# A hand-ordered transformer block on one core: bias load moved to another queue, eleven warm-ups, more softmax buffers, a new order of all steps

## The chip, the cores and the metric

The kernel runs on one core of a Trainium2 chip. The metric is device time in microseconds (us) of one execution; the median of several executions is compared. Before the change the median of three runs is 173.74 us (173.52 to 173.78).

The engines are PE (TensorE, matmuls into the eight PSUM banks), DVE (VectorE), ACT (ScalarE), POOL (GpSimd) and SP (SyncE, which here only issues DMAs). Each works through its own queue in order and waits on semaphores for the others.

## The reference

Two branches share one layer norm of `x` (2048 tokens, 512 wide) and are added to it. Weights and activations are bf16.

```python
xn = (x - mean) / sqrt(var + 1e-5)

# branch A: linear attention, 32 heads of 16, feature maps from two softmaxes
q, k, v = split(xn @ wqkv)
pq, pk  = q @ w_phi, k @ w_phi                      # per head, 16x16
phi_q   = concat([softmax(pq), softmax(-pq)])
phi_k   = concat([softmax(pk), softmax(-pk)])
kv, z   = phi_k^T v, sum(phi_k)                     # per head
o       = (phi_q @ kv) / (phi_q . z + 1e-6)
A       = o @ wo

# branch B: dense, mish, dense (hidden width 1792)
h   = xn @ w1 + b1
B   = (h * tanh(softplus(h))) @ w2

out = x + A + B
```

## The kernel before

The 2048 tokens are 16 tiles of 128, in four groups of four. `xnT` holds the normalised tokens turned, so that they can be the stationary or the moving operand of the projections. `w_phi` is folded into the weights of k and q on the chip: `wT`, the turned slice of `wqkv`, comes by a DMA transpose (L143), and 16 small matmuls per slice (F0 for k, F for q, L156) multiply it by the block-diagonal `Wbd`. Attention works in two passes: `s` from 0 to 3 for the keys of the four token groups, 4 to 7 for the queries.

All work is cut into steps, and one string, `STEPS` (L24), lists them in the order in which the kernel emits them; nothing else reorders them. Since each engine's queue runs in order, `STEPS` sets the order on each engine, and the order of DMAs on SP. `@b` names the PSUM bank that a step's result takes; a bank is free again when the copy that reads it has run. `a` or `v` at the end of a step says whether ACT or DVE does it. The steps that matter here:

- `LS i`, `RS i`, `AZ i`, `TP i`, `TC i`: the first token group tile by tile. Statistics on DVE (L170, L172), reciprocal root on POOL (L176, L177), normalise on DVE (L181), four transposes on TensorE (L560), copy to `xnT` (L565).
- `LN g`, `AP g k`: statistics and root of a later group; then two tiles normalised on DVE and one DMA transpose issued on SP for them (L186), which writes their part of `xnT`. The text calls such a DMA transpose a turn.
- `F0 kt`, `FD kt`: fold of k's weights and copy to `wkp`. `F`, `FC`: the same for q into `wqp`. `WT` loads the second `wT`.
- `LP`: the first two tiles' key logits, eight matmuls (L209). `L s i` one tile's logits (L194), `WL i` the same into a spare bank pair, `LC s i` the copy into `p_sb` (L252).
- `V t`, `VC t`: values of a tile (L194) and copy into `vext` (L218).
- `H u`, `M u`: a 128x512 block of the hidden layer (L228), mish with bias `b1f` on ACT (L239). Fourteen blocks per token group: H 0 to 13 belong to the first, H 14 to 27 to the second.
- `PB`, `CB`: the bias arrives as 14 rows of 128 in `b1b`; PB turns it on TensorE (L533), CB copies it to `b1f` (L605). All mish steps read `b1f`.
- `E s 0/1`: running maximum or minimum over 16 entries and the difference (L263 to L272, DVE). `X s k`: exponentials (L288, ACT). `S s k`: sums (L305, DVE). `R s k`: reciprocal of the sums, on DVE (L334, L335) or as exp(-ln) on ACT (L322, L314). `N s k`: normalise (L340). `A g k`: accumulate kv (L387). For queries `W s k` weighs and turns (L345), `Q`, `G`, `C` attend, gather and divide.
- `O t`, `P t`, `Y t`: second dense layer (L463), output projection (L470), residual and store (L477, L478). `OH`, `PH`, `YH`: the last tile in two parts.
- `DX g` loads a token group, `DW 2` and `DW 3` load `w2` and `wo`; all on SP.

Before the steps, DMAs are issued by hand: on SP the first x tile, `wT`, x tiles 2 and 3, `wv`, the first half of `w1`, x tiles 4 to 7, the second half of `w1`; on ACT `w_phi`, x tile 1 and the bias. Then twelve warm-up matmuls on constants (L512) keep TensorE busy while loads arrive.

The softmax sums `s` have 3 buffers (L304), `r2` has 2 (the pool's default), and logarithms go to a tile of their own (L318).

Of the kernel before, what the change touches and what calls it, by code (L numbers as in the profile page):

```python
# [21 lines left out]
STEPS = """  # L24
LS 0; RS 0; DX 2; LS 1; WB; RS 1; AZ 0; TP 0 @0; F0 0 @1; F0 1 @2; AZ 1; FD 0 v; TP 1 @3; TC 1 v; LS
2; PB @4; RS 2; TC 0 a; LS 3; RS 3; FD 1 a; AZ 2; F0 2 @5; F0 3 @0; FD 2 a; FD 3 a; LP i @1,2; KM;
DX 3; AZ 3; V 0 @3; LC 0 0 a; TP 2 @5; V 1 @0; TC 2 a; TP 3 @1; VC 0 a; LC 0 1 v; TC 3 v; CB; L 0 2
@5; L 0 3 @2; LC 0 3 a; LN 1; H 0 @3; H 1 @1; H 2 @4; M 0; LC 0 2 a; H 3 @2; M 1; M 2; M 3; VC 1 a;
E 0 0; H 4 @3; H 5 @5; AP 1 0; H 6 @1; H 7 @4; M 4; H 8 @2; M 5; H 9 @0; M 6; M 7; H 10 @3; M 8; M
9; M 10; AP 1 1; H 11 @5; E 0 1; V 4 @1; X 0 1; WL 1; LN 2; V 6 @4; VC 4 a; X 0 0; L 1 0 @2; L 1 3  # L30
@0; LC 1 0 a; V 5 @3; LN 3; VC 5 a; H 12 @1; WL 2; H 13 @2; VC 6 a; S 0 0; LC 1 3 a; M 11; V 3 @3; M
12; M 13; H 14 @4; H 15 @0; H 16 @5; H 17 @1; VC 3 a; M 14; H 18 @2; M 15; M 16; M 17; LC 1 2 a; H
19 @3; AP 2 0; AP 2 1; AP 3 0; L 2 0 @4; LC 2 0 a; L 2 1 @0; LC 2 1 a; V 2 @5; S 0 1; L 2 2 @1; M
18; LC 1 1 a; M 19; H 20 @4; LC 2 2 a; AP 3 1; H 21 @0; WT; H 22 @2; M 20; VC 2 a; R 0 1 v; L 2 3
@3; H 23 @1; R 0 0 v; N 0 1; M 21; N 0 0; H 24 @4; M 22; LC 2 3 a; F 0 @5; F 1 @0; E 1 0; E 1 1; M
23; M 24; F 2 @2; E 2 0; E 2 1; FC 0 a; H 25 @3; H 26 @1; FC 1 a; H 27 @4; M 25; M 26; L 3 2 @5; FC
2 a; M 27; V 7 @0; L 3 3 @3; V 11 @1; F 3 @2; L 3 0 @4; LC 3 0 v; LC 3 2 a; L 3 1 @5; A 0 0; X 1 0;
X 1 1; A 0 1; LC 3 3 a; FC 3 v; S 1 0; V 8 @4; LC 3 1 a; VC 7 a; L 4 0 @2; E 3 0; VC 8 a; LC 4 0 a;
L 4 1 @3; LC 4 1 a; L 4 3 @5; VC 11 a; L 4 2 @0; X 2 0; V 9 @4; L 5 0 @2; H 28 @3; H 29 @1; VC 9 a;
LC 4 2 v; M 28; M 29; H 30 @0; H 31 @4; H 32 @3; M 30; H 33 @1; H 34 @0; M 31; M 32; M 33; M 34; H  # L40
35 @4; M 35; H 36 @3; M 36; S 1 1; LC 4 3 a; R 1 0 v; E 3 1; LC 5 0 a; N 1 0; R 1 1 v; H 37 @1; H 38
@0; H 39 @4; H 40 @3; H 41 @5; H 42 @2; S 2 0; A 1 0; M 37; N 1 1; M 38; M 39; M 40; A 1 1; M 41; M
42; X 3 0; L 6 3 @1; L 5 2 @0; V 10 @4; VC 10 a; L 5 1 @3; LC 5 2 a; L 6 0 @5; E 4 0; E 4 1; X 2 1;
S 3 0; V 15 @2; VC 15 a; V 13 @4; VC 13 a; LC 6 0 a; R 2 0 a; S 2 1; DW 3; R 3 0 a; X 3 1; L 6 1 @0;
LC 5 1 a; DW 2; N 3 0; N 2 0; L 5 3 @2; O 0 @4; S 3 1; V 12 @5; V 14 @3; LC 6 1 a; LC 5 3 a; O 1 @0;
L 6 2 @2; R 2 1 a; N 2 1; VC 14 a; LC 6 3 a; VC 12 v; R 3 1 a; N 3 1; X 4 0; A 2 0; S 4 0; LC 6 2 a;
A 2 1; A 3 0; W 4 0 v; X 4 1; H 43 @3; M 43; A 3 1; H 44 @1; H 45 @5; M 44; H 46 @2; M 45; H 47 @3;
M 46; M 47; H 48 @1; KV; H 49 @5; H 50 @2; Q 0 0; M 48; M 49; G 0 0; M 50; H 51 @3; H 52 @1; H 53
@5; S 4 1; W 4 1 v; M 51; M 52; H 54 @2; H 55 @3; Q 0 1; M 53; E 5 0; E 5 1; M 54; E 6 0; L 7 0 @1;
M 55; G 0 1; C 0 a; X 5 0; LC 7 0 a; L 7 1 @5; X 5 1; O 2 @2; O 3 @3; LC 7 1 a; L 7 2 @1; LC 7 2 a;  # L50
S 5 0; Q 1 0; L 7 3 @5; G 1 0; E 6 1; W 5 0 a; P 0; P 1; Y 0; Q 1 1; O 4 @1; G 1 1; LC 7 3 a; O 5
@4; S 5 1; Q 2 0; O 6 @5; C 1 a; P 2; G 2 0; W 5 1 v; Y 1; Q 2 1; P 3; O 7 @0; E 7 0; X 6 0; S 6 0;
G 2 1; Q 3 0; C 2 a; G 3 0; Y 2; Y 3; X 6 1; O 8 @2; Q 3 1; W 6 0 v; E 7 1; S 6 1; P 4; P 5; G 3 1;
C 3 a; Q 4 0; X 7 0; Y 4; W 6 1 v; X 7 1; S 7 0; O 9 @3; O 10 @1; G 4 0; Q 4 1; P 6; P 7; G 4 1; Y
5; Y 6; C 4 a; Q 5 0; W 7 0 a; G 5 0; O 11 @4; Q 5 1; Y 7; O 12 @5; S 7 1; G 5 1; C 5 a; Q 6 0; G 6
0; O 13 @0; Q 6 1; G 6 1; W 7 1 v; P 8; P 9; Q 7 0; C 6 a; G 7 0; P 10; P 11; Y 8; Q 7 1; G 7 1; O
14 @2; Y 9; Y 10; C 7 a; P 12; P 13; OH 0 @3; PH 0; Y 11; P 14; OH 1 @1; PH 1; Y 12; Y 13; YH 0; Y
14; YH 1
"""


# [1 line left out]
def kernel(  # L63
# [424 lines left out]
    nc.scalar.dma_start(b1b[:], b1_v[:, :])  # L488
# [167 lines left out]
```

## Time and profile before

| what | value |
| --- | --- |
| median of 3 runs | 173.74 us |
| the profiled execution's own time | 174.0 us |
| its span (first to last instruction or landing on the core) | 172.3 us |
| DVE: sums of exponentials (L305) | 36.4 us busy, 16 of 2.28 us |
| ACT: mish (L239) | 37.2 us busy, 56 of 0.69 us |
| ACT: table loads (L138, L495) | 8 of 1.28 us |
| DMA: x, the three 512 KB loads, issue to landing | median 10.0 us |
| DMA: turns of xn, issue to landing | 3.3 us |

The granted TensorE clock is 1.0 in the profile's record over the whole span. An instruction's duration is longer than the distance to the next one where an engine pipelines: a 128x512 matmul lasts 0.379 us, and the next one starts 0.216 us after it; a 128x512 copy on ACT lasts 0.587 us, and the next one can start 0.48 us after it.

### The profile page before, as it was taken

The page shows a single profiled execution, that of the slowest core. Times are in us where ns is not written, and L with a number is a line of the kernel's source. Part 1 is how long each engine was busy: PE and PEld are TensorE (multiplying, and loading weights), DVE is VectorE, ACT ScalarE, POOL GpSimd, SP SyncE. Part 2 cuts the span into 40 slices and gives each one's busy share as a digit, 9 for nine tenths or more (in the row PEclk, how much of TensorE's full clock was granted, in tenths as well). Part 3 has the DMA queues.
Part 4 walks back from the last instruction along what each step waited for, and adds up shares of the span by engine and source line. Part 5 has one row for each costly group of instructions (what it writes and reads, how often), then busy time and mean ns, then how long its engine had stood idle before and what let it go on. Part 6 is the DMA issues. An engine that isn't in the chain of part 4 may idle for free.

```text
span 172.3 us, 2713 instructions
## 1 busy us (share of the span) xinstructions
PE 168.7 (98%) x1039; PEld 82.4 (48%) x1039; DVE 143.2 (83%) x221; ACT 119.5 (69%) x192; POOL 9.4 (5%) x26
## 2 busy tenths in 40 slices
PE   8999999999999999999999999999999999999993
PEld 2554444444545444454446544444444545445452
DVE  2878998999997999979999999799988996844433
ACT  2446889979899998989999988974063883414200
POOL 4332205000000000000000000000000000000000
PEclk9999999999999999999999999999999999999999
DMA  5999350199930000000000363023974749885641
GB/s 98 269 377 365 82 98 0 37 189 207 366 120 0 0 4 0 0 0 0 4 0 0 64 118 66 12 51 67 150 152 93 150 95 144 172 168 100 173 134 61
DMA packets 44953, 18.02 MB, mean 105 GB/s; under 512 B 37004, under 2 KB 44940, under 8 KB 44940
## 3 DMA queue, kind: packets, MB, share of 16 engines
q1 hardware_dynamic: 44096, 17.60, 44.5%
...
q8 instruction: 8, 0.13, 0.3%
q14 instruction: 5, 0.04, 0.1%
...
## 4 chain that ended last, share of the span: by engine, by line
PE 95%; DMA 3%; SPq 0%; DVE 0%; issue 0%
PE po L463 28%; PE ph L228 28%; PE pl L194 14%; PE po L470 8%; PE pv L194 8%; DMA wT<-in_A_wqkv_dram 3%; PE pnd L418 2%; PE pkv L387 2%; PE pfold L156 1%; PE pwide L194 1%; PE pl L209 1%; PE ptr L560 0%; SPq L483 0%; DVE x_sb L477 0%; PE pb L533 0%
## 5 line engine op out<-in xcount | busy, mean ns | idle before, releaser
L463 PE MATMUL po<-w_sb,acts 128*128 128x512 bf16 (+2 forms) x238 | 50.7, 366 | 0.0
L228 PE MATMUL ph<-xnT,w_sb 128*128 128x512 bf16 x224 | 50.1, 379 | 0.0
L239 ACT ACTIVATE acts<-ph,b1f 128x512 bf16<-128x512 f32 x56 | 37.2, 694 | 4.6 <-PE ph L228 4.4
L305 DVE TENSOR_REDUCE s<-e 128x128 f32<-128x2048 bf16 x16 | 36.4, 2279 | 2.5 <-ACT e L288 2.5
L228 PEld LDWEIGHTS <-w_sb 128*128 128x128 bf16 x224 | 21.7, 98 | 25.5
L463 PEld LDWEIGHTS <-acts 128*128 128x128 bf16 x238 | 22.3, 98 | 24.1
L288 ACT ACTIVATE e<-e 128x2048 bf16<-128x2048 bf16 x16 | 30.3, 1908 | 0.0
L194 PEld LDWEIGHTS <-xnT 128*128 128x128 bf16 x184 | 17.6, 98 | 20.1 <-DMA wv<-in_A_wqkv_dram 0.2
L252 ACT CAST p_sb<-pl 128x512 bf16<-128x512 f32 x27 | 15.4, 587 | 5.5 <-PE pl L194 4.7
L433 ACT COPY ds<-pnd 128x32 f32<-128x32 f32 x16 | 2.9, 183 | 23.5 <-PE pnd L418 23.5
L194 PE MATMUL pv<-wv,xnT 128*128 128x512 bf16 x64 | 16.1, 379 | 0.0
L477 DVE TENSOR_TENSOR x_sb<-po,x_sb 128x512 bf16<-128x512 f32 (+2 forms) x17 | 10.9, 654 | 5.7 <-PE po L470 5.7
L470 PE MATMUL po<-wqk,xnT 128*128 128x512 bf16 (+2 forms) x68 | 15.5, 366 | 0.0
L194 PE MATMUL pl<-wqk,xnT 128*128 128x512 bf16 x64 | 15.3, 379 | 0.0
L170 DVE BATCH_NORM_STATS2 stats<-x_sb 128x6 f32<-128x512 bf16 x16 | 10.1, 679 | 4.3 <-DMA x_sb<-in_A_x_dram 4.3
L263 DVE TENSOR_TENSOR m<-m 128x512 bf16<-128x512 bf16 (+1 forms) x32 | 11.5, 358 | 1.1
L194 PE MATMUL pl<-wkp,xnT 128*128 128x512 bf16 x48 | 11.7, 379 | 0.0
L263 DVE TENSOR_TENSOR m<-p_sb 128x1024 bf16<-128x1024 bf16 x16 | 10.9, 682 | 0.2 <-ACT p_sb L252 0.2
L272 DVE TENSOR_TENSOR e<-p_sb,m 128x2048 bf16<-128x2048 bf16 x8 | 9.8, 1226 | 1.4 <-PE pkv L387 1.1
L272 DVE TENSOR_TENSOR e<-m,p_sb 128x2048 bf16<-128x2048 bf16 x8 | 9.8, 1225 | 0.3
L340 DVE TENSOR_TENSOR e<-e,r 128x2048 bf16<-128x2048 bf16 x8 | 9.6, 1215 | 0.0
L138 ACT ACT_TABLE_LOAD x7 | 9.0, 1283 | 0.1
...
## 6 DMA issues: line engine op xcount, KB each, us to landing
...
x_sb<-in_A_x_dram SPq DMA_DIRECT2D x3, 512.0 KB, 10.0
...
```

Source lines behind the costliest of these rows:

```text
L170: nc.vector.bn_stats(stats[:, i, :], xs[:, i, :])
L194: nc.tensor.matmul(pp, lhsT=xnT[:, t, kt, :], rhs=w[:, kt, :], start=(kt == 0), stop=(kt == KT - 1),)
L228: nc.tensor.matmul(ph_of[u][:], lhsT=w1_sb[:, kt, f * P : (f + 1) * P], rhs=xnT[:, g * TPG : (g + 1) * TPG, kt, :], start=(kt == 0), stop= ...
L239: nc.scalar.activation(acts[:, f, g * 512 : (g + 1) * 512], ph_of.pop(u)[:], ACT.Mish, bias=b1f[:, f : f + 1])
L252: copy(p_of[s][:, i, :], pl_of.pop((s, i)))
L263: nc.vector.tensor_tensor(out=m[:], in0=src[:, :, 0:half], in1=src[:, :, half : 2 * half], op=op)
L272: nc.vector.tensor_tensor(out=e_of[s][:].rearrange("p t j l c -> p (t j) l c")[:, :, pl, :].rearrange("p t (c e o) -> p t c e o", e=8, o=2 ...
L288: nc.scalar.activation(v, v, ACT.Exp)
L305: nc.vector.reduce_sum(t[:], pair(s, k).rearrange("p t j l (c e) -> p (t j l c) e", e=16), axis=AX.X)
L463: nc.tensor.matmul(po_of[t, c.stop][:, c], lhsT=acts[:, f, t * P : (t + 1) * P], rhs=w2_sb[:, f, c], start=(f == 0), stop=False,)
L470: nc.tensor.matmul(po_of[t, c.stop][:, c], lhsT=oT_of[t // 2][:, t % 2 * 4 + j, :], rhs=wo_sb[:, j, c], start=False, stop=(j == 3),)
L477: nc.vector.tensor_tensor(out=y, in0=po_of.pop((t, c.stop))[:, c], in1=y, op=ALU.add)
```

## The change

Four edits, and with them a new `STEPS` string:

- the load of `b1b` goes from ACT's queue to SP's, between the first half of `w1` and x tiles 4 to 7;
- `WARM` is 11 instead of 12;
- `s` has 6 buffers, `r2` 3, and DVE's `r` 1;
- `log` writes its result over its input instead of a tile of its own (called by `invert`, `weigh`, `combine`);
- `STEPS`: every step occurs as often as before, in another order, with other banks, and some copies, reciprocals and weighings on the other engine. Shown are the opening up to the second group's logits, and the end.

```diff
-WARM = 12
+WARM = 11
 STEPS = """
-LS 0; RS 0; DX 2; LS 1; WB; RS 1; AZ 0; TP 0 @0; F0 0 @1; F0 1 @2; AZ 1; FD 0 v; TP 1 @3; TC 1 v; LS
-2; PB @4; RS 2; TC 0 a; LS 3; RS 3; FD 1 a; AZ 2; F0 2 @5; F0 3 @0; FD 2 a; FD 3 a; LP i @1,2; KM;
-DX 3; AZ 3; V 0 @3; LC 0 0 a; TP 2 @5; V 1 @0; TC 2 a; TP 3 @1; VC 0 a; LC 0 1 v; TC 3 v; CB; L 0 2
-@5; L 0 3 @2; LC 0 3 a; LN 1; H 0 @3; H 1 @1; H 2 @4; M 0; LC 0 2 a; H 3 @2; M 1; M 2; M 3; VC 1 a;
-E 0 0; H 4 @3; H 5 @5; AP 1 0; H 6 @1; H 7 @4; M 4; H 8 @2; M 5; H 9 @0; M 6; M 7; H 10 @3; M 8; M
-9; M 10; AP 1 1; H 11 @5; E 0 1; V 4 @1; X 0 1; WL 1; LN 2; V 6 @4; VC 4 a; X 0 0; L 1 0 @2; L 1 3
...
+LS 0; LS 1; RS 0; AZ 0; TP 0 @0; WB; F0 0 @1; RS 1; AZ 1; TP 1 @2; F0 1 @3; FD 0 a; TC 0 v; F0 2 @4;
+FD 1 a; FD 2 a; TC 1 v; LS 2; F0 3 @5; FD 3 v; LP i @0,1; LS 3; RS 2; LC 0 0 a; RS 3; V 1 @2; AZ 2;
+TP 2 @3; AZ 3; V 0 @4; TP 3 @5; DX 2; TC 2 a; L 0 2 @0; VC 0 a; PB @3; TC 3 v; L 0 3 @4; VC 1 a; H 0
+@5; LC 0 3 a; H 1 @2; CB; LC 0 2 a; M 0; M 1; H 2 @3; M 2; LN 1; LN 2; AP 1 0; AP 1 1; H 3 @4; H 4
+@0; H 5 @5; AP 2 0; H 6 @2; M 3; H 7 @3; M 4; M 5; M 6; M 7; DX 3; LC 0 1 a; E 0 0; E 0 1; H 8 @4; H
+9 @0; M 8; H 10 @5; H 11 @2; H 12 @3; AP 2 1; H 13 @1; M 9; H 14 @4; M 10; M 11; M 12; L 1 0 @0; M
+13; V 3 @5; M 14; X 0 1; LN 3; L 2 0 @2; S 0 1; LC 1 0 v; X 0 0; WL 1; S 0 0; L 2 1 @3; V 2 @1; WL
+2; L 2 2 @4; LC 2 0 a; LC 2 1 a; LC 2 2 a; VC 3 a; H 15 @2; H 16 @3; R 0 1 a; AP 3 0; L 2 3 @0; M
...
+@2; C 7 v; OH 0 @5; P 12; P 13; PH 0; P 14; OH 1 @1; PH 1; Y 11; Y 12; Y 13; YH 0; Y 14; YH 1
 """
@@ sums
-        t = s_of[s, k] = smx.tile([P, 128], FP32, name="s", bufs=3)
+        t = s_of[s, k] = smx.tile([P, 128], FP32, name="s", bufs=6)
@@ log
-    def log(src, n):
+    def log(v):
 
         table("natural_log_exp_and_others")
-        t = smx.tile([P, 128], FP32, name="log")
-        nc.scalar.activation(t[:, 0:n], src, ACT.Ln)
-        return t[:, 0:n]
+        nc.scalar.activation(v, v, ACT.Ln)
+        return v
@@ invert
-        r2 = r_of[s, k] = smx.tile([P, 128, 2], BF16, name="r2")
+        r2 = r_of[s, k] = smx.tile([P, 128, 2], BF16, name="r2", bufs=3)
         if how == "a":
-            power(r2[:], log(t[:], 128), 128, -1.0)
+            power(r2[:], log(t[:]), 128, -1.0)
             return
-        r = smx.tile([P, 128], BF16, name="r")
+        r = smx.tile([P, 128], BF16, name="r", bufs=1)
@@ DMAs ahead of the steps
     nc.scalar.dma_start(x_sb[:, 1, :], x_v[:, 1, :])
-    nc.scalar.dma_start(b1b[:], b1_v[:, :])
     nc.sync.dma_start(x_sb[:, 2:4, :], x_v[:, 2:4, :])
     nc.sync.dma_start(wv[:], wqkv_v[:, :, 2 * D : 3 * D])
     nc.sync.dma_start(w1_sb[:, :, 0 : 7 * P], w1_v[:, :, 0 : 7 * P])
+    nc.sync.dma_start(b1b[:], b1_v[:, :])
     nc.sync.dma_start(x_sb[:, 4:8, :], x_v[:, 4:8, :])
     nc.sync.dma_start(w1_sb[:, :, 7 * P : F], w1_v[:, :, 7 * P : F])
```

In the new order `WB` (the block-diagonal weights, on DVE, L524) stands behind `AZ 0`; the key folds' copies go to ACT for kt 0 to 2 and to DVE for kt 3; `PB` stands between `L 0 2` and `L 0 3`; `LN 2` stands ahead of `AP 1`; and SP issues x tiles 12 to 15 (`DX 3`) behind the turns of `AP 1 0`, `AP 1 1` and `AP 2 0`.

More of the change, by code (lines that the diff above doesn't have):

```diff
@@ L30 @@
-9; M 10; AP 1 1; H 11 @5; E 0 1; V 4 @1; X 0 1; WL 1; LN 2; V 6 @4; VC 4 a; X 0 0; L 1 0 @2; L 1 3
[L31 to L58, printed above, removed]
+LS 0; LS 1; RS 0; AZ 0; TP 0 @0; WB; F0 0 @1; RS 1; AZ 1; TP 1 @2; F0 1 @3; FD 0 a; TC 0 v; F0 2 @4;
+FD 1 a; FD 2 a; TC 1 v; LS 2; F0 3 @5; FD 3 v; LP i @0,1; LS 3; RS 2; LC 0 0 a; RS 3; V 1 @2; AZ 2;
@@ new lines @@
+2; L 2 2 @4; LC 2 0 a; LC 2 1 a; LC 2 2 a; VC 3 a; H 15 @2; H 16 @3; R 0 1 a; AP 3 0; L 2 3 @0; M
+15; L 1 3 @4; AP 3 1; LC 2 3 a; LC 1 2 a; LC 1 3 a; H 17 @5; H 18 @2; H 19 @0; H 20 @4; E 2 0; N 0
+1; WT; R 0 0 v; M 16; LC 1 1 a; M 17; M 18; M 19; H 21 @3; H 22 @5; M 20; M 21; H 23 @2; M 22; M 23;
+H 24 @0; M 24; H 25 @4; H 26 @3; H 27 @5; H 28 @2; M 25; M 26; M 27; V 6 @0; VC 2 a; E 1 0; M 28; V
+5 @4; F 0 @3; E 1 1; F 1 @5; VC 6 a; F 2 @1; FC 0 a; FC 2 a; VC 5 v; H 29 @2; M 29; E 2 1; FC 1 a; V
@@ new lines @@
+9 @0; X 1 0; F 3 @4; V 10 @3; FC 3 v; N 0 0; L 3 3 @1; L 3 0 @2; X 1 1; V 8 @5; LC 3 0 v; V 7 @4; VC
+7 a; A 0 0; A 0 1; VC 10 a; V 4 @2; S 1 0; L 4 0 @4; X 2 0; VC 4 a; LC 3 3 v; LC 4 0 v; VC 9 a; S 1
+1; R 1 0 a; L 4 2 @3; LC 4 2 a; N 1 0; L 3 2 @1; LC 3 2 a; L 3 1 @4; LC 3 1 v; L 4 1 @2; L 4 3 @0; R
+1 1 v; VC 8 a; H 30 @3; H 31 @1; LC 4 3 v; H 32 @5; H 33 @4; N 1 1; X 2 1; M 30; A 1 0; M 31; E 3 0;
+S 2 0; S 2 1; M 32; M 33; H 34 @0; M 34; V 13 @3; VC 13 a; H 35 @1; H 36 @5; H 37 @4; H 38 @0; M 35;
@@ new lines @@
+M 36; M 37; LC 4 1 a; E 3 1; H 39 @3; M 38; H 40 @1; H 41 @5; M 39; H 42 @4; H 43 @2; M 40; M 41; M
+42; M 43; H 44 @0; DW 2; M 44; A 1 1; E 4 0; V 14 @3; V 11 @1; E 4 1; X 3 1; L 5 0 @5; LC 5 0 a; X 3
+0; L 5 3 @4; LC 5 3 a; R 2 1 a; O 0 @2; S 3 1; R 2 0 a; L 5 1 @0; VC 14 a; LC 5 1 a; N 2 1; VC 11 a;
+V 15 @5; VC 15 a; R 3 1 a; L 6 3 @4; S 3 0; O 1 @3; L 6 0 @0; V 12 @1; X 4 0; L 5 2 @5; N 3 1; LC 6
+0 a; R 3 0 a; N 2 0; VC 12 a; L 6 1 @0; N 3 0; LC 6 3 a; A 2 0; S 4 0; LC 5 2 a; W 4 0 v; A 2 1; DW
@@ new lines @@
+3; X 4 1; S 4 1; A 3 0; H 45 @1; A 3 1; KM; LC 6 1 a; H 46 @4; L 6 2 @5; M 45; KV; M 46; H 47 @0; H
+48 @1; M 47; LC 6 2 a; H 49 @4; M 48; M 49; W 4 1 v; H 50 @0; H 51 @5; M 50; E 5 0; M 51; E 5 1; H
+52 @1; H 53 @4; H 54 @0; M 52; M 53; E 6 0; M 54; Q 0 0; G 0 0; H 55 @5; L 7 2 @1; Q 0 1; M 55; G 0
+1; L 7 0 @4; O 2 @0; X 5 0; S 5 0; C 0 a; W 5 0 v; Q 1 0; G 1 0; O 3 @5; LC 7 0 a; LC 7 2 a; Q 1 1;
+L 7 1 @4; G 1 1; C 1 a; O 4 @1; LC 7 1 a; E 6 1; X 5 1; O 5 @4; S 5 1; P 0; Q 2 0; G 2 0; X 6 0; P
@@ new lines @@
+1; Y 0; W 5 1 v; Y 1; P 2; Q 2 1; G 2 1; P 3; S 6 0; X 6 1; L 7 3 @2; O 6 @3; Q 3 0; Y 2; W 6 0 a; O
+7 @0; LC 7 3 a; E 7 0; Y 3; G 3 0; Q 3 1; C 2 a; G 3 1; C 3 a; S 6 1; E 7 1; O 8 @2; O 9 @5; Q 4 0;
+G 4 0; P 4; P 5; W 6 1 a; Y 4; X 7 0; Y 5; P 6; P 7; Q 4 1; S 7 0; Y 6; G 4 1; O 10 @1; C 4 a; X 7
+1; Q 5 0; W 7 0 a; G 5 0; S 7 1; O 11 @4; Q 5 1; G 5 1; O 12 @3; Y 7; Q 6 0; O 13 @0; C 5 a; G 6 0;
+Q 6 1; P 8; P 9; W 7 1 v; G 6 1; C 6 v; Y 8; Q 7 0; G 7 0; Y 9; P 10; Y 10; P 11; Q 7 1; G 7 1; O 14
@@ L350, in weigh @@
         if how == "a":
-            t4 = log(t[:], 128).rearrange("p (t l c) -> p t l c", l=2, c=4)
+            t4 = log(t[:]).rearrange("p (t l c) -> p t l c", l=2, c=4)
             nc.vector.tensor_tensor(
@@ L446, in combine @@
         if how == "a":
-            power(f[:], log(d, 64), 64, -1.0)
+            power(f[:], log(d), 64, -1.0)
         else:
```

## The prediction

> **What bounds the kernel now.** I read the page's first lines, then what TensorE waited for, then the chain that ended last, and then the opening microseconds engine by engine.
>
> ```profile
> span 172.3 us, 2713 instructions
> ...
> PE 168.7 (98%) x1039; PEld 82.4 (48%) x1039; DVE 143.2 (83%) x221; ACT 119.5 (69%) x192; POOL 9.4 (5%) x26
> ```
>
> TensorE has work in 98% of the span, so the other engines matter only where they make it wait. Its list of waits has one line:
>
> ```profile
> PE warm L513 <- PEq L640: 0.8, 1, 0.8
> ```
>
> The chain, in order of time (start, length, what), says the same:
>
> ```profile
> 1.25 5.36 DMA wT<-in_A_wqkv_dram
> ...
> 6.65 0.62 PE pfold L156 x8
> ...
> 13.78 10.36 PE ph L228 x48
> ...
> 169.41 0.24 PE po L470 x4
> ...
> 169.67 0.29 DVE x_sb L477
> ```
>
> The turned weights wT, asked for at 1.25, arrive at 1.25+5.36 = 6.61. From the first fold at 6.65 to 169.65 TensorE runs piece after piece: 163.0 us. The last add, its store and the close take 172.3-169.65 = 2.65. So the span is 6.65 + 163.0 + 2.65. A new order can only start the 163.0 earlier, shorten the tail, or put a hole into the 163.0. The opening, from the timeline (start, length, engine, line):
>
> ```profile
> 0.83 5.28 PE L513 MATMUL warm<-const-bfloat16-1.0 128*128 128x512 bf16 x12 [0.83 <-PEq L640]
> 1.25 3.12 SPq L143 DMA_TRANSPOSE wT<-in_A_wqkv_dram  x1
> 1.83 0.67 ACTq L488 DMA_DIRECT2D b1b<-in_B_b_dram  x1
> 4.41 0.69 DVE L170 BATCH_NORM_STATS2 stats<-x_sb 128x6 f32<-128x512 bf16 x1 [0.32 <-DMA x_sb<-in_A_x_dram]
> 5.57 0.41 DVE L181 TENSOR_SCALAR xn<-x_sb,mv,rstd 128x512 bf16<-128x512 bf16 x1
> 5.82 0.60 POOL L177 TENSOR_TENSOR rstd<-rstd,mhalf 128x1 f32<-128x1 f32 x1
> 6.45 0.41 DVE L181 TENSOR_SCALAR xn<-x_sb,mv,rstd 128x512 bf16<-128x512 bf16 x1 [0.48 <-POOL rstd L177]
> 7.43 0.18 PE L533 MATMUL pb<-ident,b1b 14*128 14x14 bf16 x1
> 13.43 2.47 DVE L170 BATCH_NORM_STATS2 stats<-x_sb 128x6 f32<-128x512 bf16 x4 [0.83 <-DMA x_sb<-in_A_x_dram]
> ```
>
> Two things hold TensorE here: wT at 6.61, and the second token tile, whose loads end near 4.4, whose root ends on POOL at 6.42, and whose normalised copy ends at 6.86.
>
> **The change, part by part.** TensorE's real work is the same multiset of matmuls, so the 163.0 stays except for holes.
>
> *Warm-ups.* Twelve take 12 x 0.427 = 5.12 from 0.83, to 5.95; eleven end at 5.52. The first transpose (TP 0) waits for the first normalised tile: in the new DVE order WB stands behind it, so it starts 0.33 earlier, at 5.24, and ends at 5.65. But TP 0 then ends near 6.1 and the fold still waits for 6.61. Removed work lies before that wait: worth nothing by itself.
>
> *Folds, logits, values.* With wT at 6.61: fold 0 6.65 to 6.87; TP 1 (its tile ready at about 6.7 to 6.86) to 7.1; three folds of 0.222 to 7.76. The copies of folds 0 to 2 run on ACT from 7.08 at 0.48 apart and end at 7.65, 8.13 and 8.60; that of fold 3 on DVE ends near 9.1. Eight matmuls of 0.216 from 7.76 would end at 9.49; the last copies hold them to about 9.55. Before, this stretch ended at 9.72, because the bias transpose (PB) cost 0.21 between TP 1 and fold 2 (matmul starts of 7.28 and 7.54, where back to back they stand 0.06 apart) and the logits then had to wait for nothing more. Gain 0.17, not more: the values need wv, which its landing of 4.5 us after issue at 5.04 puts at 9.5.
>
> *Bias behind w1's first half.* PB moves to between L 0 2 and L 0 3, where nothing else is late, so its 0.21 is all exposed: sum so far -0.17+0.21 = +0.04. It now needs b1b. Landings follow SP's order of issue in the trace (by its landing records w1's first half at 11.9 and the next x at 13.4, which released DVE in the last line of the timeline above). So b1b lands between 11.9 and 13.4; I take 12.0, right behind w1, since 3.5 KB adds no time. TensorE reaches PB at 9.55 + 2 x 0.864 + 2 x 0.222 + 0.864 = 12.6: cost 0, and at the far end 0.8. Queued behind PB are L 0 3 and all hidden blocks. On SP the load adds one issue of about 0.5 before x 4 to 7, w1's second half and x 8 to 11; these stream without a gap, so the issue is hidden. x 12 to 15 (DX 3) is now asked for on SP behind three turns of xn, and LN 3 waits for it on DVE, with S 0 1, LC 1 0 and all that follows queued behind.
>
> *What the early queues gain.* While b1b was being asked for on ACT, wT came slowly; later its rate was much higher (start:end, length, busy, clock, DMA share, GB/s):
>
> ```profile
> 3.50:4.00 0.50, 0.50 (x3) 0.15 (x1) 0.47 (x2) 0.32 (x1) 0.00 (x0) 1.00 1.02 90
> 4.00:4.50 0.50, 0.50 (x2) 0.15 (x1) 0.18 (x2) 0.00 (x0) 0.23 (x2) 1.00 1.07 161
> 5.00:5.50 0.50, 0.50 (x3) 0.15 (x1) 0.47 (x3) 0.00 (x0) 0.16 (x2) 1.00 1.28 290
> ```
>
> If b1b caused that, wT regains (290-90)x0.5 + (290-161)x0.5 = 165 KB, or 0.57 us at 290 GB/s; the low end is 0. Whatever wT regains, TP 1 still waits for the second tile near 6.7, so TensorE gains 0.17 at most while x 1 lands at 4.39. I take a third, -0.05: the trace shows the slow stretch, not its cause. The Trainium skill speaks against any gain (page "DMA: Bandwidth & Descriptors", section "Issuing engines are not separate DMA queues"): transfers started from different engines share the same 16 DMA engines, and only the starting sequencer's time is saved. By it this term would be 0 and the forecast 0.05 later; the trace does show both queues at work in one stretch, but not which held the other.
>
> *The new order from 13 to 36 us.* I laid the rows end to end, each engine in its new order. Three handovers are tight.
> H 14 needs both turns of tokens 4 to 7. LN 2 now stands ahead of AP 1 and waits for x 8 to 11: its load, issued at 7.36 and 10.0 long (the page's median of the three 512 KB loads), lands at 17.4. LN takes 2.67 (13.43 to 16.10), so AP 1 starts at 20.05; its second turn is issued at 22.1, lands 3.3 later at 25.4. TensorE reaches H 14 at about 13.65 + 14 x 0.864 = 25.75: 0.3 spare.
> L 2 2 needs the second turn of tokens 8 to 11: LN 2's end 20.1, root 1.85 (16.27 to 18.12), two centres 0.73, E 0 0 and E 0 1 at 2.95 each, two centres, 29.3; plus 3.0 to 3.3: 32.3 to 32.6. TensorE arrives at 25.75 + 8 x 0.864 = 32.66: nothing to spare at one end.
> L 2 3 needs the bank that LC 1 0 frees on DVE behind LN 3, and LN 3 needs x 12 to 15, issued at 24.6. A lone 512 KB load lands 4.5 to 4.6 after issue (wv, wo), at 29.2, as DVE gets there; then 2.67 + 2.2 + 0.69 = 34.8, against TensorE's 35.25.
> The turns' landings spread from 3.0 to 4.8 in the trace, so holes here cost between 0 and 1.5+; I take 0.05. After 36 us no handover has less than about 0.35.
>
> *Six sum buffers, three r2, logarithms in place.* In-place logarithms are the same 0.32 and 0.27 rows. More buffers take waits from DVE, but TensorE waited for DVE nowhere after 9 us: worth 0, hidden by the 163.0. DVE keeps its load: two casts of 0.6 for each L334/L335 pair of 1.18 that moves to ACT. The tail ends in the same adds and stores: 0.
>
> Sum: -0.17 + 0.21 - 0.05 + 0.05 = +0.04 on the profiled span of 172.3. That run took 174.0, the median of the three is 173.74; I forecast 173.7, no change that can be measured. What a measurement of this kernel can tell is about 0.2%, or 0.35 us.
>
> **The rivals.**
> *Early loads come sooner as a whole.* If b1b held x 1 as well as wT (x 1 was issued on ACT just ahead of it and landed at 4.39, 3.1 after issue, against 2.4 for x 0), the root of tile 1 ends 0.3 to 0.4 sooner, every load behind wT follows, and TensorE gains up to 0.17+0.3: 173.3. For it: the 90 GB/s stretch. Against it: the first tile itself is only ready at 5.65, and b1b is 3.5 KB.
> *A late hand-over makes holes: slower.* Its place is the three turns and loads above, or PB; it decides once a turn takes 3.6 or x 12 to 15 lands after 29.6. A turn at 3.8 costs 0.35 at H 14 and as much again at L 2 2; x 12 to 15 late by 1 us costs 0.6. Together 174.5. For it: DVE, TensorE and SP stand in one chain there, which before had E 0 work between. Against: most turns were within 0.1 of 3.3.
> *The clock opens later: slower.* Warm-ups run at 0.427, real matmuls at 0.216; the array speeded up between 6.33 and 6.65, after 5.5 us of almost unbroken work. With eleven, TensorE idles 0.13 before TP 0 and 0.55 after it. If it must make up the missing 0.43, the loss is half of it, 0.2; if it needs another 5.5 us from 6.65, half of those, 2.75. Near the middle: 175.2. Against: from 0.83 to 6.65 TensorE is still busy for 5.14 of 5.82. The Trainium skill ("TensorE: Matmul & The Clock Gate", section "What's actually happening") has a free-running window of about 3.4 us that must be busy, time and not a count of matmuls; by it one missed window costs about 1.7, an estimate from that page. The granted clock in the profile reads 1.00 even during the warm-ups, so the trace can't decide it.
>
> **How the numbers follow.** Forecast, no measurable change: 0.48 (own range 173.4 to 174.05). Sooner loads, 173.3: 0.22. Holes, 174.5: 0.21. Clock, 175.2: 0.09. So faster 0.22, same 0.48, slower 0.30. The range leaves most of the clock case and the ends of the others out: 173.2 to 174.7.
>
> **What would show it.** Right: the first fold starts at 6.4 to 6.65; PB costs about 0.2 near 12.6; TensorE shows no wait over 0.1 from there to the end; and PE's chain is again about 163 us long. The sooner loads would show as wT landing before 6.2 and x 1 before 4.1. Holes would show in TensorE's waits as xnT at L228 or L194, the clock as folds 0.11 apart instead of 0.056 after 6.65. I am wrong altogether if a wait of TensorE over 0.35 stands behind 36 us, since I counted none there.

## The result and the profile after

The change makes the kernel slower by a quarter of a per cent: median 174.12 us (173.82 to 174.89), against 173.86 (173.51 to 174.27) for the kernel before, ratio 1.0023 with a 95% interval of 1.0012 to 1.0034. The profiled run took 174.6 with a span of 172.9, where before's took 174.0 with 172.3; after's profile is thus of one of its longer runs, 0.48 above its median. Line numbers of after are one or two below those of before (L194 is now L193, L560 L558, L533 L531, L186 L185, L228 L227).

TensorE's busy share and its list of waits after the change (line, what was waited for, us in total, times, longest):

```profile
span 172.9 us, 2710 instructions
...
PE 168.8 (98%) x1038; PEld 82.3 (48%) x1038; DVE 144.2 (83%) x224; ACT 118.7 (69%) x190; POOL 9.0 (5%) x26
```

```profile
PE warm L511 <- PEq L638: 0.8, 1, 0.8
PE pfold L155 <- DMA wT<-in_A_wqkv_dram: 0.3, 1, 0.3
PE ph L227 <- DMA xnT<-xn: 0.2, 1, 0.2
```

TensorE still bounds the kernel, but a hidden block now waits for a turn of xn. TensorE runs from 6.57 to 170.24, 163.67 instead of 163.0, and the tail is 2.66 as before. So 0.67 of new holes stand against a first fold that starts 0.08 sooner. They lie in three places. First the opening, in TensorE's timeline (start, length, engine, line):

```profile
6.57 0.40 PE L155 MATMUL pfold<-Wbd,wT 128*128 128x128 bf16 x4 [0.27 <-DMA wT<-in_A_wqkv_dram]
7.03 0.40 PE L558 MATMUL ptr<-ident,xn 128*128 128x128 bf16 x4
7.26 0.83 PE L155 MATMUL pfold<-Wbd,wT 128*128 128x128 bf16 x12
7.93 2.00 PE L208 MATMUL pl<-wkp,xnT 128*128 128x512 bf16 x8
9.76 0.59 PE L193 MATMUL pv<-wv,xnT 128*128 128x512 bf16 x2
```

The last two of these groups before:

```profile
8.00 1.89 PE L209 MATMUL pl<-wkp,xnT 128*128 128x512 bf16 x8
9.72 0.59 PE L194 MATMUL pv<-wv,xnT 128*128 128x512 bf16 x2
```

PB has gone from between TP 1 and the folds, yet the logits start only 0.07 sooner and the values 0.04 later. Two waits have taken its place, and both show on DVE in after:

```profile
6.56 0.41 DVE L180 TENSOR_SCALAR xn<-x_sb,mv,rstd 128x512 bf16<-128x512 bf16 x1 [0.48 <-POOL rstd L176]
8.62 0.66 DVE L164 CAST wkp<-pfold 128x512 bf16<-128x512 f32 x1
```

The first stands ahead of TP 1. In before TP 1 follows two folds, 0.46 after the first fold starts; in after it follows one, comes due 0.23 after it, and must wait for the second tile's centre, which ends at 6.97. It starts at 7.03, again 0.46 after the first fold, so TensorE now spends on this wait the 0.2 that PB took, and from the first fold to the logits are 1.36 in after and 1.35 in before. The second is fold 3's copy, which stands behind LS 2 on DVE and ends at 9.28: the seventh of the eight logit matmuls starts 0.31 after the sixth instead of 0.22, at 9.33.

Second, PB in its new place, after:

```profile
11.94 1.03 PE L193 MATMUL pl<-wkp,xnT 128*128 128x512 bf16 x4
12.89 0.18 PE L531 MATMUL pb<-ident,b1b 14*128 14x14 bf16 x1
13.00 1.04 PE L193 MATMUL pl<-wkp,xnT 128*128 128x512 bf16 x4
```

From 11.94 to 13.00 are 1.06 for four matmuls that take 0.86: PB costs the 0.2 in full. Third, the hole of 0.33 ahead of H 14 (26.30 instead of 25.97), whose history stands in the chain of waits, in order of time:

```profile
7.91 9.79 DMA x_sb<-in_A_x_dram
...
17.73 2.47 DVE stats L169 x4
...
22.04 0.43 DVE xn L180 x2
22.47 3.70 DMA xnT<-xn
26.30 1.02 PE ph L227 x4
```

x 8 to 11 lands at 17.70, LN 2 holds DVE behind it, only then can the roots and centres of AP 1 follow, and the second turn lands 3.70 after its issue, at 26.16. The first turn, issued at 21.13, took 4.19.

### The profile page after: what moved, and what is told of

The parts are those of the page before. It is cut to its first block, busy times and chain, and to the rows that moved or that the text cites. A ratio compares the mean times of both kernels' runs of the same rounds, so it can differ in the third digit from the quotient of the medians.

```text
span 172.9 us, 2710 instructions
## 1 busy us (share of the span) xinstructions
PE 168.8 (98%) x1038; PEld 82.3 (48%) x1038; DVE 144.2 (83%) x224; ACT 118.7 (69%) x190; POOL 9.0 (5%) x26
## 4 chain that ended last, share of the span: by engine, by line
PE 83%; DMA 8%; SPq 4%; DVE 2%; POOL 1%; issue 0%
PE po L461 28%; PE ph L227 21%; PE pl L193 13%; PE po L468 8%; PE pv L193 7%; DMA x_sb<-in_A_x_dram 6%; PE pnd L416 2%; PE pkv L385 2%; DMA xnT<-xn 2%; SPq L142 2%; DVE stats L169 1%; PE pwide L193 1%; POOL rstd L176 1%; PE pfold L155 1%; SPq L491 0%
## 5 line engine op out<-in xcount | busy, mean ns | idle before, releaser
L227 PE MATMUL ph<-xnT,w_sb 128*128 128x512 bf16 x224 | 50.3, 379 | 0.2 <-DMA xnT<-xn 0.2
L227 PEld LDWEIGHTS <-w_sb 128*128 128x128 bf16 x224 | 21.6, 98 | 25.6 <-issue 0.6
L193 PEld LDWEIGHTS <-xnT 128*128 128x128 bf16 x184 | 17.5, 98 | 19.8
L193 PE MATMUL pv<-wv,xnT 128*128 128x512 bf16 x64 | 15.9, 379 | 0.0
L251 ACT CAST p_sb<-pl 128x512 bf16<-128x512 f32 x24 | 13.5, 584 | 3.4 <-PE pl L193 2.4
L193 PE MATMUL pl<-wqk,xnT 128*128 128x512 bf16 x64 | 15.8, 379 | 0.0
L193 PE MATMUL pl<-wkp,xnT 128*128 128x512 bf16 x48 | 11.8, 379 | 0.0
L468 PEld LDWEIGHTS <-xnT 128*128 128x128 bf16 x68 | 6.2, 98 | 6.1
```

The source lines that it names most:

```text
L193: nc.tensor.matmul(pp, lhsT=xnT[:, t, kt, :], rhs=w[:, kt, :], start=(kt == 0), stop=(kt == KT - 1),)
L227: nc.tensor.matmul(ph_of[u][:], lhsT=w1_sb[:, kt, f * P : (f + 1) * P], rhs=xnT[:, g * TPG : (g + 1) * TPG, kt, :], start=(kt == 0), stop= ...
L251: copy(p_of[s][:, i, :], pl_of.pop((s, i)))
L468: nc.tensor.matmul(po_of[t, c.stop][:, c], lhsT=oT_of[t // 2][:, t % 2 * 4 + j, :], rhs=wo_sb[:, j, c], start=False, stop=(j == 3),)
```

## The experiments

Each is compared with the kernel before on the same chip. They fall into four groups, one chip each (xf, pb, v3, warm12; again, pad10, xfpad10, bpad2; pbpad10, xfpbpad10, bbias, bpb; swap, swapopen, bswap, bbuf), and the unchanged after was measured beside others in the second alone. Three sections of TensorE's timeline keep the causes apart: the start of the first values, the time from there to the first hidden block, and the time from that to TensorE's last matmul.

| kernel | first values | to first hidden block | from there to the end | ratio to before (95%) |
| --- | --- | --- | --- | --- |
| before | 9.72 | 3.90 | 156.02 | |
| after | 9.76 | 4.12 | 156.35 | 1.0023 (1.0012 to 1.0034) |
| again (after) | 9.39 | 4.12 | 156.45 | 1.0028 (1.0018 to 1.0038) |
| warm12 | 9.69 | 4.12 | 156.27 | 1.0040 (1.0027 to 1.0053) |
| v3 | 9.44 | 4.11 | 156.41 | 1.0041 (1.0028 to 1.0054) |
| pb | 9.66 | 3.90 | 156.52 | 1.0060 (1.0046 to 1.0074) |
| xf | 9.95 | 4.11 | 156.01 | 1.0013 (1.0004 to 1.0022) |
| pad10 | 9.72 | 4.12 | 156.02 | 1.0018 (1.0009 to 1.0027) |
| xfpad10 | 9.55 | 4.11 | 156.01 | 1.0017 (1.0006 to 1.0029) |
| pbpad10 | 9.40 | 3.90 | 156.02 | 1.0011 (1.0001 to 1.0021) |
| xfpbpad10 | 9.59 | 3.90 | 156.02 | 1.0003 (0.9994 to 1.0011) |
| swap | 9.76 | 3.90 | 156.01 | 1.0001 (0.9993 to 1.0010) |
| swapopen | 9.90 | 4.53 | 156.02 | 1.0086 (1.0054 to 1.0117) |
| bbias | 9.67 | 4.13 | 156.02 | 1.0010 (1.0002 to 1.0019) |
| bpb | 9.70 | 3.90 | 156.01 | 0.9998 (0.9989 to 1.0006) |
| bpad2 | 9.60 | 3.91 | 156.06 | 0.9997 (0.9989 to 1.0006) |
| bbuf | 9.37 | 3.91 | 156.01 | 0.9996 (0.9986 to 1.0005) |
| bswap | 9.52 | 3.89 | 156.07 | 0.9995 (0.9986 to 1.0003) |

The first column moves by 0.6 with the landings, from run to run of one kernel too (after 9.76 and 9.39). In xf LS 2, ahead of fold 3's copy, waited for x 2 and 3 until 7.96. The second is 3.90 or 4.12 and nothing else, but for swapopen. The third is 156.0 to 156.1 in both orders wherever neither H 14 nor, in v3, H 15 waits. Beside LS 2 in xf, the values themselves waited in bbias, for wv until 9.63.

**xf: x 8 to 11 sooner.**

```diff
     nc.sync.dma_start(x_sb[:, 4:8, :], x_v[:, 4:8, :])
+    nc.sync.dma_start(x_sb[:, 8:12, :], x_v[:, 8:12, :])
     nc.sync.dma_start(w1_sb[:, :, 7 * P : F], w1_v[:, :, 7 * P : F])
...
-TP 2 @3; AZ 3; V 0 @4; TP 3 @5; DX 2; TC 2 a;
+TP 2 @3; AZ 3; V 0 @4; TP 3 @5; TC 2 a;
```

> After with one load moved: x tiles 8 to 11 are asked for behind x 4 to 7 and ahead of the second half of w1, by hand; the step DX 2 goes. Nothing else changes. T1 (the lost time is one chain: x 8 to 11 lands at 17.70, LN 2 stands ahead of AP 1 on DVE and idles 1.07 for it, the second turn lands at 26.16 and H 14 waits until 26.30): x 8 to 11 lands at 15.0 to 16.0, LN 2 starts at about 16.66 as DVE comes to it, the second turn lands near 25.1, the hole of 0.33 ahead of H 14 is gone, and the median falls by 0.2 to 0.4 below after, to 173.75 to 173.95, with a narrower spread. T2 (the bias part costs it: its load and PB's exposed 0.21): no change, 174.0 to 174.2, since both stay. T3 (eleven warm-ups cost it): no change. Against T1 would also be a new wait for w1's second half, which lands later, near 17.5, and which H 7 first needs near 19.9.

x 8 to 11 landed at 14.99, the second turn was issued at 20.89 instead of 22.47 and landed at 25.03; H 14 did not wait. The ratio is 1.0013, and 1.0040 and 1.0041 for warm12 and v3 beside it. The hole ahead of H 14 is where T1 put it. But the second turn took 4.14, so earlier loads are not the whole of it: a turn was slow here as well, the second and not, as in after, the first.

**pb: the bias part undone.**

```diff
-LS 0; LS 1; RS 0; AZ 0; TP 0 @0; WB; F0 0 @1; RS 1; AZ 1; TP 1 @2; F0 1 @3; FD 0 a; TC 0 v; F0 2 @4;
+LS 0; LS 1; RS 0; AZ 0; TP 0 @0; PB @4; CB; WB; F0 0 @1; RS 1; AZ 1; TP 1 @2; F0 1 @3; FD 0 a; TC 0
...
+    nc.scalar.dma_start(b1b[:], b1_v[:, :])
...
-    nc.sync.dma_start(b1b[:], b1_v[:, :])
...
-        "CB": lambda: nc.vector.tensor_copy(b1f[:], pf_of.pop("b")[:, 0:FT]),
+        "CB": lambda: nc.scalar.copy(b1f[:], pf_of.pop("b")[:, 0:FT]),
```

> After with the bias part undone: its load goes back to ACT's queue behind x tile 1, and PB and its copy (on ACT instead of DVE) stand right behind TP 0, where TensorE waits for wT. T2 (the bias behind w1 delays the x loads by one issue each and exposes PB's 0.21): PB's time is hidden, x 8 to 11 lands 0.3 earlier, near 17.4, and the median falls by 0.25 to 0.4, to about 173.75. T1 (H 14 waits for LN 2 behind x 8 to 11): TensorE reaches H 14 0.2 sooner and waits as much longer, except for what the earlier landing gives, so a gain of 0 to 0.15 only and a hole of 0.2 to 0.5 ahead of H 14 in the profile. T3 (warm-ups): no change. If b1b lands on ACT's queue later than wT, PB holds the fold and the opening loses up to 0.2.

Slower than every other new order but one, 1.0060, and no theory had that. From the list of TensorE's waits in pb:

```profile
PE ph L227 <- DMA xnT<-xn: 0.3, 1, 0.3
```

PB's 0.21 is gone (3.90), and the wait ahead of H 14 has grown: its matmuls start at 25.43 and 26.15, a hole of 0.50. Its timed runs (up to 175.29) are longer than its profiled one (174.43), and by what is not shown.

**v3: work ahead of H 14.**

```diff
-9 @0; M 8; H 10 @5; H 11 @2; H 12 @3; AP 2 1; H 13 @1; M 9; H 14 @4; M 10; M 11; M 12; L 1 0 @0; M
-13; V 3 @5; M 14; X 0 1; LN 3; L 2 0 @2; S 0 1; LC 1 0 v; X 0 0; WL 1; S 0 0; L 2 1 @3; V 2 @1; WL
+9 @0; M 8; H 10 @5; H 11 @2; H 12 @3; AP 2 1; H 13 @1; M 9; V 3 @5; H 14 @4; M 10; M 11; M 12; L 1 0
+@0; M 13; M 14; X 0 1; LN 3; L 2 0 @2; S 0 1; LC 1 0 v; X 0 0; WL 1; S 0 0; L 2 1 @3; V 2 @1; WL 2;
```

> After with one step of TensorE moved: V 3 (four matmuls of 0.216, which need nothing late) goes from behind H 14 and L 1 0 to just ahead of H 14. T1: the hole of 0.33 ahead of H 14 is filled, L 2 2 and X 0 1 stand behind the same landing and take up part of it: a gain of 0.1 to 0.33, 173.8 to 174.0, and the hole of H 14 below 0.1. T2 and T3: no change, 174.1. If V 3's copy now holds a bank that H 14 or L 2 0 needs, slower by 0.1 to 0.3.

No gain. The hole at H 14 is filled, and in its stead stands one of 0.38 (matmul starts of 33.20 and 33.80): H 15 waits for a bank that ACT frees late. The wait, and the chain that leads to it:

```profile
PE ph L227 <- ACT p_sb L251: 0.2, 1, 0.2
```

```profile
26.67 0.88 PE ph L227 x4
...
27.57 0.69 ACT acts L238
...
29.57 3.71 ACT e L287 x2
33.28 0.48 ACT p_sb L251
```

The second hole is the move's own. V 3 takes 0.86, more than the hole that it fills, so H 14 starts at 26.67, though its turn had landed at 26.02. M 14 on ACT can only start when H 14 is through, and behind it, in ACT's order, stand a table load, two exponentials and the copy that frees H 15's bank. A step put ahead of a late one delays all that hangs on the late one, by as much as it is longer than the hole.

**warm12: twelve warm-ups.** `WARM = 12` in after, nothing else.

> After with twelve warm-ups instead of eleven, nothing else. T3 (with eleven TensorE is slow for longer, or wakes later): the median falls by 0.2 or more. T1 and T2: the twelfth ends at 5.95 and pushes TP 0 back by 0.4, but the first fold still waits for wT near 6.55, so no change: 174.0 to 174.2.

1.0040, with 1.0041 for v3 beside it: nothing comes back. The folds stand 0.056 apart from the first one on with eleven as with twelve. T3 is out.

**again: after once more.** It is the measure for the group beside it.

> After once more, unchanged, as the measure for the other runs beside it. Every theory: 173.9 to 174.6. T1 (H 14 waits for a turn behind x 8 to 11) and T4 (the turns are held up for 0.75 us by something that follows an 8 KB fetch of instructions at about 23.8) expect a hole of 0.2 to 0.5 ahead of H 14 again, T4 also a fetch within 1 us of 23.9 and a turn of about 4.2 from issue to landing.

174.40, ratio 1.0028, the hole of 0.42 ahead of H 14 (25.38 to 26.02), and a first turn of 4.21.

**pad10: ten instructions ahead of DVE's work.** What xf and after had in common was found in the packet records: the turns' packets all but stop for 0.75 us, and in every run this began 0.3 after a packet of 8,192 bytes on the queue of instruction fetches (23.91 in after, 23.72 in xf, 24.54 in pb, which has one DVE instruction less ahead of it).

```diff
+    spare = consts.tile([P, 16], FP32, name="spare")
...
     nc.scalar.preload_act_table_set("mish")
+    for i in range(10):
+        nc.vector.memset(spare[:, i : i + 1], 0.0)
```

> After with ten memsets of one column each on DVE at the very start, where DVE waits for x (until 2.95), so nothing else is later. They push DVE's code on by ten instructions. T4 (DVE fetches its next 8 KB of code at its 48th to 50th instruction, and the turns in flight stand still for 0.75 us from 0.3 us after it): the fetch comes ten instructions sooner, at 20 to 21, ahead of the turns' packets; the three turns land 3.2 to 3.5 after issue, the second near 25.7, the hole ahead of H 14 is under 0.1, and the median falls 0.3 to 0.7 below the unchanged kernel beside it. T1 (only x 8 to 11 and LN 2 set it): the turns stay at 4.2 or the hole stays, no change. If the fetch does not move by ten instructions it is not DVE's, and nothing follows of T4's cause.

DMA rates from 20 to 28 us in 40 slices of 0.2, and the turns' median from issue to landing, first of after, then of pad10:

```profile
GB/s 0 0 0 0 0 0 0 0 0 0 0 47 220 223 206 212 191 176 89 264 207 141 37 8 8 180 291 272 293 284 256 210 189 120 184 333 364 256 338 374
...
xnT<-xn SPq DMA_TRANSPOSE x3, 3.7
```

```profile
GB/s 0 0 0 0 0 0 0 0 41 0 13 170 212 206 73 159 282 217 175 220 206 204 215 175 130 214 221 214 205 206 160 95 151 61 143 271 241 256 364 369
...
xnT<-xn SPq DMA_TRANSPOSE x3, 3.2
```

In after the rate falls from 207 to 8 between 24.2 and 25.0 (141, 37, 8, 8) with three turns under way. In pad10 the fetch stands at 21.78 (the single 41), ahead of the turns' packets, and that stretch is gone; another fetch moved from 113.4 to 107.1, and those near 38, 142 and 152 stayed. The turns take 3.22, 3.38 and 3.20, and TensorE's list of waits has no line for `ph` or `xnT` any more.

The fetch came sooner by 2 us, not by all ten instructions: 49 of DVE's records (its sequencer's included) start before it in after, and 54 in pad10, ten of them the memsets. Without memsets the count is 47 to 50 in every kernel, with ten it is 53 or 54. So the fetch keeps near to a place in DVE's program, but not to one exact count, which is what the expectation had asked for: that it is DVE's is likely, not shown. The median is 0.17 below that of again beside it (174.23 against 174.40), less than forecast, and the two intervals overlap; the hole is closed in the trace, its worth in the median not resolved by this pair.

**xfpad10: both.** xf and the ten memsets.

> After with both: x 8 to 11 loaded ahead of w1's second half, and the ten memsets. T1 and T4 each take one delay out: turns issued about 19.6 and 20.9. With both the second turn lands near 24.2, 2 us ahead of H 14; if T4 is right and the fetch (about 20.3) falls before the first turn's packets, all turns take 3.2 to 3.5 and the median is the lowest of this call, 173.6 to 173.9. If T4 is wrong, as xf: 174.0 to 174.2. If the fetch now comes between 20.9 and 23.5, a turn takes 4.2 all the same, with slack enough to hide it at H 14.

No hole, turns of 3.25, 3.32 and 3.13, fetch at 20.68; but 174.17, 1.0017, which is no better than xf. What is left is not at H 14.

**bpad2: two memsets in before.**

> Before with two memsets of one column on DVE at the start. In before the fetch came at 23.81, when the last packets of the two turns (issued 19.80 and 21.15) had gone, and the turns took 3.4. T4: two instructions sooner is 22.2 to 23.3, and the second turn's packets stand still for about 0.75; it lands near 25.3 instead of 24.55, still ahead of H 14 at 25.7, so the time stays within 0.1 of before, 173.8 to 174.0, but the trace shows the stall. If the fetch moves and no turn slows, T4's mechanism falls.

No change in time, 0.9997. The fetch stayed at 23.77, since x 8 to 11 landed half a microsecond later in that run and DVE with it; but the second turn, issued at 21.69, was now under way then, its rate fell to 8 GB/s, and it took 3.90 where before's took 3.40. So the old order has the same stall within reach. The first step that reads this turn there is V 6, at 25.71 in before, 1.16 after the landing; in bpad2 the turn landed at 25.59 and V 6 started at 25.64, with hardly any slack left.

**pbpad10 and xfpbpad10: every suspected cost out.** pb with the ten memsets; and that with xf's load.

> After with the bias part undone (as in pb: loaded on ACT's queue, PB right behind TP 0 in the wait for wT, copied by ACT) and the ten memsets at DVE's start. T4 plus an exposed PB (the theory now: 0.21 of PB and 0.2 to 0.5 of a hole ahead of H 14 make the loss): both terms are out, the first hidden block starts at 13.4 to 13.65, TensorE then needs 156.0 to its end as in before, no wait ahead of H 14, and the ratio to before is 0.999 to 1.001; pb without the memsets stood at 1.006. Rival T5 (something of the new order after 36 us, or of the six buffers, costs it): no hole ahead of H 14 but more than 156.2 from the first hidden block to the end, ratio 1.002 or more.

> pbpad10 with x tiles 8 to 11 loaded ahead of w1's second half as well, so that the turns are issued about 1.1 sooner and land 1 to 2 ahead of H 14. T4 plus PB: as pbpad10 with less spread, ratio 0.998 to 1.0005, the best of the new orders. T5: 1.002 or more.

pb went from 1.0060 to 1.0011 with ten memsets, its hole from 0.50 to none. The two were measured on different chips, each against before on its own. xfpbpad10 stands at 1.0003 and its spread (173.76 to 174.40) is close to that of before beside it (173.69 to 174.19); its list of waits has one line, the start. So the new order, the buffers and the logarithms as a whole cost nothing that this comparison resolves (0.9994 to 1.0011) once PB is hidden and the turns have slack; T5 falls. Seven of pbpad10's twelve runs still lie at 174.15 to 174.47, and its profile (of the fastest, 173.66) cannot say why; with earlier loads one of eleven does.

**bbias and bpb: the bias alone, in before.** In bbias the load goes to SP behind w1's first half and PB and CB between L 0 2 and L 0 3; in bpb PB goes to right behind TP 0.

```diff
-2; PB @4; RS 2; TC 0 a; LS 3; RS 3; FD 1 a; AZ 2; F0 2 @5; F0 3 @0; FD 2 a; FD 3 a; LP i @1,2; KM;
+2; RS 2; TC 0 a; LS 3; RS 3; FD 1 a; AZ 2; F0 2 @5; F0 3 @0; FD 2 a; FD 3 a; LP i @1,2; KM; DX 3; AZ
...
+3; V 0 @3; LC 0 0 a; TP 2 @5; V 1 @0; TC 2 a; TP 3 @1; VC 0 a; LC 0 1 v; TC 3 v; L 0 2 @5; PB @4;
```

> Before with the bias part of the change alone: b1b on SP behind w1's first half, PB and its copy between L 0 2 and L 0 3. If PB's 0.21 is only moved from one exposed place to another, no change: ratio 0.999 to 1.001, V starting 0.1 to 0.2 sooner and the first hidden block at 13.5 to 13.7. If it is hidden in the old place or the load pushes x 4 to 7 back: 1.001 to 1.002. If b1b on ACT's queue had held wT or x 1 up: wT lands before 6.3, x 1 before 4.1 and the ratio is under 0.999.

> Before with PB moved from between TP 1 and fold 2 to right behind TP 0, into the wait for wT, its copy on ACT. If PB's 0.21 is exposed in before: V starts 0.1 to 0.2 sooner and the ratio is 0.9985 to 0.9995. If the second tile (not TensorE's own work) sets the opening: no change, 0.9995 to 1.0005. If b1b lands after 6.3 on ACT's queue, PB holds the first fold and it is slower by up to 0.2.

bbias is 0.23 slower in the median (174.15 against 173.92; 0.03 to 0.33 by its interval), and its timeline shows where, PB between two tiles' logits:

```profile
11.86 1.03 PE L194 MATMUL pl<-wkp,xnT 128*128 128x512 bf16 x4
12.82 0.18 PE L533 MATMUL pb<-ident,b1b 14*128 14x14 bf16 x1
12.93 1.04 PE L194 MATMUL pl<-wkp,xnT 128*128 128x512 bf16 x4
```

bpb, where PB is hidden beyond doubt, gains nothing over before. Its first two logits, then those of before, and the copy that the second of them needs, on bpb's DVE:

```profile
7.84 0.72 PE L209 MATMUL pl<-wkp,xnT 128*128 128x512 bf16 x2
```

```profile
8.00 0.59 PE L209 MATMUL pl<-wkp,xnT 128*128 128x512 bf16 x2
```

```profile
7.71 0.41 DVE L565 COPY xnT<-ptr 128x512 bf16<-128x512 bf16 x1
```

Without PB ahead of them the logits start 0.16 sooner, but the two then take 0.72 instead of 0.59, because the second belongs to the second tile and waits for TC 1 (8.12), which stands behind fold 0's copy on DVE: of the 0.16, 0.03 is left. So PB was hidden in before and is exposed in after. The bias part alone, load and PB together, is worth 0.23 in the median, of the size of what the change lost in the main comparison (0.26).

**swap, swapopen, bswap: is the opening set by x 1?** x 1 is asked for ahead of `w_phi` on ACT's queue, in xfpbpad10 (swap) and in bpb (bswap); swapopen also moves three steps:

```diff
-TP 0 @0; PB @4; CB; WB; F0 0 @1; RS 1; AZ 1; TP 1 @2; F0 1 @3; FD 0 a; TC 0
+TP 0 @0; PB @4; CB; WB; RS 1; AZ 1; TP 1 @2; F0 0 @1; F0 1 @3; FD 0 a; TC 0
...
-LS 2; F0 3 @5; FD 3 v;
+F0 3 @5; FD 3 v; LS 2;
...
-V 1 @2; AZ 2; TP 2 @3; AZ 3; V 0 @4; TP 3 @5;
+V 1 @2; AZ 2; V 0 @4; TP 2 @3; AZ 3; TP 3 @5;
```

> xfpbpad10 (ratio to before 1.0003) with x tile 1 asked for ahead of w_phi on ACT's queue. If the second tile sets the opening: x 1 lands near 3.2 instead of 4.35, the second centre ends at about 6.2 instead of 6.8, no wait of TP 1 for xn; but fold 3's copy still stands behind LS 2, which needs x 2 and 3 (7.5), so V starts only 0 to 0.1 sooner and the ratio is 0.999 to 1.0005. If wv (9.2 to 9.5) or the array sets it: no change in V. If w_phi now comes late for WB (before 5.5): slower by up to 0.2.

> swap with three steps moved: TP 1 ahead of the first fold, fold 3's copy ahead of LS 2 on DVE, V 0 ahead of TP 2. If the second tile and then LS 2 set the opening: folds follow wT without a gap, fold 3's copy ends near 8.0 instead of 9.1, the logits end at 9.2 or so and V starts as wv lands (9.2 to 9.5); 0.2 to 0.35 is gained in the opening and the ratio is 0.9975 to 0.999, faster than before. If the later LS 2 makes TP 2 late by as much: no gain, 0.9995 to 1.0005.

> bpb (before with PB in the wait for wT; ratio 0.9998) with x tile 1 asked for ahead of w_phi. If the second tile sets before's opening: TP 1 at 6.7 to 6.9 instead of 7.12, V 0.1 to 0.2 sooner, ratio 0.998 to 0.9995. If not: 0.9995 to 1.0005.

x 1 landed at 3.95 and not near 3.2, and x 0 at 3.72 instead of about 3.0: asked for at the same moment, the two landed within 0.25 of each other, tile 0 came later, and swap's values start at 9.76. The test of x 1 failed in that form. bswap's 0.9995 is within its interval of no change. swapopen lost 1.1 us: the first fold now waits for TP 1, and LS 2 behind fold 3's copy makes TP 2 and the copy of its tile late:

```profile
PE ptr L562 <- DVE xn L181: 0.6, 2, 0.4
PE pl L194 <- ACT xnT L567: 0.4, 1, 0.4
```

The kernels that ask for x 1 in its old place tell more, and they say that the two orders hang on different loads. In the old order TP 1 follows two folds and starts 0.46 after the first fold in all of before, bbuf, bpb, bpad2 and bbias, with x 1 landing at 4.09 to 4.39; the values start 3.04 to 3.12 after the first fold (3.21 in bbias, behind wv). So the old opening hangs on wT, and in bswap, with x 1 at 3.98, both distances are the same, 0.46 and 3.04. In the new order TP 1 starts 2.51 to 2.57 after x 1's landing in eight of ten kernels and waits for it; the values start 3.16 to 3.33 after the first fold there (3.55 in xf). Only in again and pbpad10, where x 1 landed at 3.99 and 4.03, does TP 1 follow the first fold without a wait, and the values then start 2.96 after it. So x 1 sets the new opening and not the old one, and with x 1's usual landing the new opening is some 0.1 to 0.25 longer than the old one, counted from wT.

**bbuf: buffers and logarithms alone, in before.** The hunks of `sums`, `log` and `invert` of the change.

> Before with the buffers and the logarithms of the change alone: six s, three r2, one r, log in place; order, bias and warm-ups as before. Forecast of the prediction: worth nothing, ratio 0.9993 to 1.0007, 156.0 from the first hidden block to the end. If they cost (a wait for the one r, or a log that waits for its input's readers): over 156.2 there and a ratio over 1.001.

0.9996 and 156.01: worth nothing, as forecast.

No kernel beats before by what a measurement can tell.

## Why the prediction was wrong

*Warm-ups: 0, right.* TP 0 did not start at 5.24, though, but at 5.80: in the new order AZ 0 stands behind LS 1, which waits for x 1. The fold waits for wT until 6.5 anyway.

*Folds, logits, values: -0.17, the step that failed.* It read "Before, this stretch ended at 9.72, because the bias transpose (PB) cost 0.21 between TP 1 and fold 2". The gap between matmul starts at PB was real, but taking PB out gained nothing in either order. In the old order the second logit matmul then waits for TC 1, which the sum left out: bpb gains 0.02 (9.70). In the new order TensorE waits 0.23 ahead of TP 1 instead. The prediction had that wait in view and took the second tile as ready at 6.7 to 6.86 and TP 1 as done by 7.1; x 1 landed at 4.51, the centre ended at 6.97, and TP 1 started at 7.03. Fold 3's copy ended at 9.28 instead of 9.1. Measured: +0.04.

*PB in its new place: +0.21, right.* 4.12 instead of 3.90 in every kernel that has it there. Set against a gain of 0, it makes a loss.

*Early queues: -0.05, not resolved.* wT landed at 6.52 with b1b on SP, and in the other kernels at 6.17 to 6.49 with it there, against 6.25 to 6.62 with it on ACT; x 1 at 3.99 to 4.51 and 4.03 to 4.41. These ranges overlap; the means of wT, 6.37 and 6.43, differ by 0.06 within spreads of 0.35. The rule of the Trainium skill that was weighed against this term ("DMA: Bandwidth & Descriptors", "Issuing engines are not separate DMA queues") gave 0, and these landings cannot tell 0 from 0.05. The rival of loads that come sooner as a whole falls: x 1 came no sooner with b1b on SP, and in after it landed at 4.51.

*Holes from 13 to 36 us: +0.05, mis-sized.* The place, H 14, and its spare of 0.3 were named. x 8 to 11 landed at 17.70 instead of 17.4, so the turn was issued 0.37 late, and it took 3.70 instead of 3.3: it landed at 26.16 instead of 25.4, and the hole was 0.33 (again: 0.42). The rival "a late hand-over makes holes" is what happened, at its price for H 14; a hole at L 2 2 came in none of these traces. The slow turn was taken for spread; it has a time of its own, 0.3 after an 8 KB instruction fetch.

*After 36 us: no wait, right.* *Buffers and logarithms: 0, right.* *The clock opens later: refuted* by warm12.

The sum of the profile: 0.04 in the opening, 0.22 to the first hidden block, 0.33 ahead of H 14, 0.59 in all against 0.6 measured. Of the 0.55 by which this exceeds the forecast of 0.04, the hole accounts for 0.28, and the opening (forecast as -0.17 and -0.05) for 0.26. In the median the loss is 0.26 in the main comparison and 0.50 in again. The first is little more than the 0.23 that bbias lost by the bias part; the times of after spread over 1.07 us, those of before over 0.76, which fits a hole that comes and goes with the landings but was not traced run by run.
